# A recurrent-memory attention loop: the second softmax product split over two engines, a V copy moved ahead of a product, and one group of Q sums moved

## The chip, the cores and the metric

The kernel runs on one core of a Trainium2 chip. The metric is device time in microseconds (us) of one execution, compared as the median of several. Five engines matter: PE (TensorE, matmuls; its weight loads are shown as PEld), DVE (VectorE), ACT (ScalarE), POOL (GpSimd) and SP (SyncE, which issues the DMAs). Each runs its own instructions in order; they wait for each other by semaphores.

## The reference

The input of 2048 rows of 512 is normalised and cut into 64 segments of 32 rows. Each segment is attended to by 32 heads of 128 together with 8 memory rows, and the first 8 rows of the attention's output are the memory of the next segment, so the segments run one after the other. Behind it comes a gated MLP with a mixing over the 2048 rows.

```python
mem = mem0
for s in range(n_seg):
    h = concatenate([mem, xs], axis=1)
    q, k, v = h @ Wq, h @ Wk, h @ Wv            # 32 heads of 128
    p = softmax(where(mask, q @ k.T * scale, -1e9))
    o = (p @ v) @ Wo
    mem = o[:, :M, :]
    outs.append(o[:, M:, :])
# then: z = gelu(x @ w_in); g = w_sp @ layernorm(z2) + b_sp; out = (z1 * g) @ w_out
```

## The kernel before

**A list of operations.** Python code adds operations to an emitter, each with the tokens it reads and writes (`("E", b)` is the softmax numerator of head half `b`, `("V", b, h)` a half of that half's V). The emitter works out which semaphores an operation must wait for. An instruction carries one wait; each further wait is an instruction of its own on that engine. Each engine runs its operations in the order in which they were added. A POOL operation always waits for the POOL operation ahead of it.

**One segment.** The loop `for s in range(NSEG)` adds one segment at a time. The 32 heads are worked as two halves, `b` = 0 and 1, of 16. The large products on PE are split in fours: four matmuls, one in each column quarter of the array, for one 128-row chunk `dc` of the 512 input columns; a four of 512 columns costs PE one stream of 512 columns. When two fours that follow one another use the same chunk, the second keeps ("holds") the weights of the first (they show under line 501 instead of 500). In program order a segment is:

1. `QK` (through `tile_mm`, lines 500 and 501): fours for the Q and K sums. `QK(s, b, mi, dcs, first, last, held)` adds the fours of half `b`, `mi` 0 for Q and 1 for K, chunks `dcs`. Chunks 0 and 1 need the first half of the mem rows, chunks 2 and 3 the second.
2. In the middle of them `mem_out(s - 1, 1)` (line 702) transposes the second half of the last segment's mem rows with tiny matmuls; an ACT copy (line 707) puts them where the fours of chunks 2 and 3 read them.
3. `QK_evac`: ACT copies a finished PSUM bank to `Tst` (line 537), DVE transposes it into `QT` or `KT` (line 549). `mask_put` (DVE, line 561) writes the mask into the score bank. `K1` sums K of the second half in two 256-column parts, with `K1_copy` on ACT (line 527) and `K1_transpose` on DVE (line 534).
4. `S_half(s, b)` (lines 571 and 577): scores; `sm_exp` on ACT (line 585); `V_half` fours; `sm_sums` (lines 592, 501); `sm_ln` and `sm_rcp` on ACT (lines 603, 607) give the reciprocal `R`.
5. The softmax product `sm_norm` multiplies the first 160 columns of `E` by `R` (line 611), `sm_normx` the 64 columns of the ext part, which belong to the memory rows' neighbours of a whole row block (line 617, always DVE). `V_evac` copies V out of PSUM (DVE line 637, ACT line 635). An operation that reads a PSUM bank waits for another engine's read of that bank that was added before.
6. Filler work for PE (sums for later segments, lines 437, 418, 500 with `hTe`, or 797), then `PV_half(s, 0)` and `PV_half(s, 1)`: 16 small matmuls (line 645) and 4 for the ext part (line 651, which also read `Vx`, loaded by DMA a segment ahead), `cT_evac`, the output product `Wo`, `part_evac`, `mem_out(s, 0)`.

The order of step 5 is written out by hand: `sm_norm(0)` on POOL, then on DVE `sm_normx(0)`, `V_evac(1, (0,))`, `sm_norm(1)`, `sm_normx(1)`, with the other half of V's copy on ACT.

**The planner.** PE's instructions come in blocks of 256 (`FETCH`). `plan` looks four segments ahead, works out where in each segment a block ends, gives penalties to some places (`weight_of`), and chooses how many of a segment's fours reload weights instead of holding them, four more instructions each, to move the ends. `WAITS` and a term per segment count the separate wait instructions.

Of the kernel before, what the change touches and what calls it, by code (L numbers as in the profile page):

```python
# [10 lines left out]
ALU = mybir.AluOpType  # L11
# [158 lines left out]
def fast_path(nc, st, keep, A_x, A_mem0, A_Wq, A_Wk, A_Wv, A_Wo, A_seg_len, B_w_in, B_w_sp, B_b_sp, B_w_out, out):  # L170
# [9 lines left out]
    DC = D // 128  # L180
# [16 lines left out]
    def sb(name, shape, dt):  # L197
        return st.enter_context(nc.sbuf_tensor("f_" + name, shape, dt))
# [23 lines left out]
    NVX = 3  # L222
    Vx = sb("Vx", [128, NVX, 2, 128], BF)
    Vs = sb("Vs", [128, 2, 512], BF)
    E_sb = sb("E_sb", [128, 2, 224], BF)
    R_sb = sb("R_sb", [128, 2, 160], F32)
# [9 lines left out]
    ones = sb("ones", [128, 128], BF)  # L236
# [30 lines left out]
    def PB(b):  # L267
        return ("ps", b)
# [4 lines left out]
    pe_count = [0]  # L273
# [214 lines left out]
    PVB = (0, 1, 6, 7)  # L488
# [17 lines left out]
    def QK(s, b, mi, dcs, first, last, held=None):  # L506
        ws = (w_q, w_k)[mi]
        bank = QKB[(b, mi)]
        sl = slot(s)
        for dc in dcs:  # L510
            for c in range(4):
                rhs = ws[:, dc, :].rearrange("p (h c i) -> p c h i", c=4, i=32)[:, c, 16 * b:16 * b + 16, :]
                pe(lambda e, dc=dc, c=c, rhs=rhs: tile_mm(e, ps[32 * c:32 * c + 32, bank, :], hT[:, sl, dc, :], rhs,
                                                          dc == first, dc == last, c, dc == held), n=2 - (dc == held),
                   reads=[("hTx", (s // 4) % 3), ("hTm", s, dc // 2), ("W", mi, 2 * b), ("W", mi, 2 * b + 1)], writes=[PB(bank)])
# [67 lines left out]
    def sm_exp(b):  # L583
        bank = SBK[b]
        act(lambda e: e.activation(out=E_sb[:, b, :], in_=ps[:, bank, 0:224], func=ACT.Exp, scale=scale, bias=SHIFT),  # L585
            reads=[PB(bank)], writes=[("E", b), ("Ex", b)])

    def sm_sums(b):
        bank = SBK[b]
        for c in range(4):  # L590
            q = slice(32 * c, 32 * c + 32)
            pe(lambda e, q=q, c=c: e.matmul(ps[q, bank, 224:384], lhsT=ones[:, q], rhs=E_sb[:, b, 0:160], start=True, stop=False,  # L592
                                            skip_group_check=True, tile_position=(0, 32 * c)),
               reads=[("E", b), "ones"], writes=[PB(bank)])
        for c in range(4):
            q = slice(32 * c, 32 * c + 32)
            pe(lambda e, q=q, c=c: tile_mm(e, ps[q, bank, 224:384].rearrange("p (g q) -> p g q", q=40)[:, :, 0:16], ones[:, q],
                                           E_sb[:, b, 160:224].rearrange("p (g q) -> p g q", q=16), False, True, c, True), n=1,
               reads=[("Ex", b), "ones"], writes=[PB(bank)])
# [7 lines left out]
        act(lambda e: e.activation(out=R_sb[:, b, :], in_=R_sb[:, b, :], func=ACT.Exp, scale=-1.0, bias=RBIAS),  # L607
            reads=[("R", b)], writes=[("R", b)])

    def sm_norm(b, on):  # L610
        on(lambda e: e.tensor_tensor(out=E_sb[:, b, 0:160], in0=R_sb[:, b, :], in1=E_sb[:, b, 0:160], op=ALU.mult),
           reads=[("R", b), ("E", b)], writes=[("E", b)])

    def sm_normx(b):
        ev = E_sb[:, b, 160:224].rearrange("p (g q) -> p g q", q=16)
        rv = R_sb[:, b, :].rearrange("p (g q) -> p g q", q=40)[:, :, 0:16]
        dve(lambda e: e.tensor_tensor(out=ev, in0=rv, in1=ev, op=ALU.mult), reads=[("R", b), ("Ex", b)], writes=[("Ex", b)])

    def V_half(s, b, dcs=range(DC), held=None):
        bank = VB[b]  # L620
        sl = slot(s)
        last = 2 if b and s else DC - 1
        for dc in dcs:
            for c in range(4):
                c0 = (16 * b + 4 * c) * DH
                pe(lambda e, dc=dc, c=c, c0=c0: tile_mm(e, ps[32 * c:32 * c + 32, bank, :], hT[:, sl, dc, :], w_v[:, dc, c0:c0 + 512],
                                                        dc == 0, dc == last, c, dc == held), n=2 - (dc == held),
                   reads=[("hTx", (s // 4) % 3), ("hTm", s, dc // 2), ("W", 2, 2 * b), ("W", 2, 2 * b + 1)], writes=[PB(bank)])

    def V_evac(b, hs=(0, 1), eng="dve"):  # L630
        bank = VB[b]
        cs = slice(256 * hs[0], 256 * hs[-1] + 256)
        wr = [("V", b, h) for h in hs]
        if eng == "act":
            act(lambda e: e.activation(out=V_sb[:, b, cs], in_=ps[:, bank, cs], func=ACT.Copy), reads=[PB(bank)], writes=wr)
        else:
            dve(lambda e: e.tensor_copy(out=V_sb[:, b, cs], in_=ps[:, bank, cs]), reads=[PB(bank)], writes=wr)  # L637

    def PV_half(s, b):
        xb = s % NVX  # L640
        for g in range(4):
            for c in range(4):
                q = slice(32 * c, 32 * c + 32)
                c0 = 160 * b + 40 * g
                pe(lambda e, q=q, c=c, g=g, c0=c0: e.matmul(  # L645
                    ps[:, PVB[c], c0:c0 + 40], lhsT=V_sb[q, b, g * 128:(g + 1) * 128], rhs=E_sb[q, b, g * 40:(g + 1) * 40],
                    start=(g == 0), stop=False, skip_group_check=True, tile_position=(32 * c, 0)),
                    reads=[("V", b, g // 2), ("E", b)], writes=[PB(PVB[c])])
        for c in range(4):
            q = slice(32 * c, 32 * c + 32)  # L650
            pe(lambda e, q=q, c=c: e.matmul(  # L651
                ps[:, PVB[c], 160 * b:160 * b + 160].rearrange("p (g q) -> p g q", q=40)[:, :, 0:16], lhsT=Vx[q, xb, b, :],
                rhs=E_sb[q, b, 160:224].rearrange("p (g q) -> p g q", q=16),
                start=False, stop=True, skip_group_check=True, tile_position=(32 * c, 0)),
                reads=[("Vx", xb), ("Ex", b)], writes=[PB(PVB[c])])
# [41 lines left out]
    def mem_out(s, half):  # L697
        bank = GB[half]
        for dc in range(2 * half, 2 * half + 2):
            for c in range(4):  # L700
                c0 = dc * 128 + 32 * c
                pe(lambda e, dc=dc, c=c, c0=c0: e.matmul(ps[32 * c:32 * c + 32, bank, dc * M:(dc + 1) * M], lhsT=part[:, s % 8, c0:c0 + 32],  # L702
                                                         rhs=G_sb[:, :], start=True, stop=True, skip_group_check=True, tile_position=(0, 32 * c)),
                   reads=[("part", s % 8, half), "G"], writes=[PB(bank)])
        d2 = slice(2 * half, 2 * half + 2)
        src = ps[:, bank, 2 * half * M:(2 * half + 2) * M].rearrange("p (dc c) -> p dc c", c=M)
        act(lambda e: e.activation(out=hT[:, slot(s + 1), d2, 0:M], in_=src, func=ACT.Copy),  # L707
            reads=[PB(bank)], writes=[("hTm", s + 1, half)])
# [292 lines left out]
           reads=[("z2p", r, hf) for r in range(r0, r1) for hf in range(2)],  # L1001
           writes=[("z2", r, hf) for r in range(r0, r1) for hf in range(2)], after=[after])

    FETCH, FETCH0, WAITS = 256, 191, 15
    spare = [0]

    def weight_of(place):
# [6 lines left out]
    def plan(s, start, depth=4):  # L1014
        n = 588 + 24 * (s % 4 == 2) + 8 * (s >= 3 * CK)
        best = None
        for k in range(9):
            c = 10 * block_cost(start, 4 * k, n) + k
            if depth > 1:
                c += plan(s + 1, start + n + 4 * k + 2, depth - 1)[0]  # L1020
            if best is None or c < best[0]:
                best = (c, k)
        return best

    def hold(x):
        if spare[0] > 0:
            spare[0] -= 1
            return None
        return x
# [5 lines left out]
    for s in range(NSEG):  # L1035
# [12 lines left out]
        if s == 4:  # L1048
            load_xe(3, 1)

        spare[0] = plan(s, pe_count[0] + WAITS + 2 * s)[1] if s else 0
        QK(s, 0, 0, (0,), 0, 3)
        QK(s, 0, 1, (0,), 0, 2, hold(0))
        if s > 0:
            mem_out(s - 1, 1)
        QK(s, 0, 1, (1,), 0, 2)
        QK(s, 0, 0, (1, 2, 3), 0, 3, hold(1))
        QK_evac(s, 0, 0)
# [1 line left out]
        QK(s, 0, 1, (3, 2), 0, 2, hold(3))  # L1060
        QK_evac(s, 0, 1)
        mask_put(1)
        QK(s, 1, 0, (2, 0, 1, 3), 2, 3, hold(2))
        lastop["q"] = em.by_eng["pe"][-1]
        QK_evac(s, 1, 0)
        K1(s, 0, 3, True, False, bool(hold(True)))
# [35 lines left out]
        if s == 0:  # L1102
            for n in range(2, 4):
                start_v(n)
            V_half(s, 1)
            sm_sums(1)
        else:
            V_half(s, 1, (3, 1), 3)
            sm_sums(1)
            V_half(s, 1, (2,))  # L1110
        lastop["v"] = em.by_eng["pe"][-1]
        sm_ln(1)
        sm_rcp(1)
# [8 lines left out]
        if s + 1 < NSEG:  # L1122
            qx_copy(s + 1)
            lastop["x"] = xops[s + 1] = em.by_eng["pool"][-1]
        sm_norm(0, pool)
        sm_normx(0)
        V_evac(1, (0,))
        V_evac(1, (1,), "act")
        sm_norm(1, dve)
        sm_normx(1)  # L1130
        if s == 0:
            for n in range(4, 8):
# [90 lines left out]
        if c2 + 8 <= s < c3:  # L1223
            k, m = (s - c2 - 8) // 2, s % 2
# [6 lines left out]
        if s in (c3 + 5, c3 + 7, c3 + 11, c3 + 13):  # L1231
            dc = (c3 + 5, c3 + 7, c3 + 11, c3 + 13).index(s)
# [203 lines left out]
    for tb in range(NTB):  # L1436
        for fb in range(len(ACC) if tb == 0 else 0, FB):
            if tb == 0:
                bank = 5 + fb % 3
            else:  # L1440
                bank = gcnt % 2
# [786 lines left out]
```

## Time and profile before

| | us |
|---|---|
| median of 3 runs (lowest, highest) | 845.12 (843.77, 845.2) |
| the profiled execution | 842.99 |
| its span, first to last instruction | 841.3 |
| PE busy in the span | 827.7 (98%) |
| DVE busy | 524.0 (62%) |
| ACT busy | 469.1 (56%) |
| POOL busy | 127.4 (15%) |

Timeline rows read: start in us, length in us, engine, line, operation, output and inputs, how many instructions were merged, and in brackets how long the engine idled before and what ended that. Where several instructions are merged, the length is from the first's start to the last's end. Rows of groups by line read: line, engine, operation, names, shape, count, then busy time in us, mean of one in ns and idle time before them. The ends of matmuls are modelled, and matmuls overlap, so their spacing is read from start to start. The granted TensorE clock is 1.000 throughout.

### The profile page before, as it was taken

The numbers are of one execution on the slowest core, as the hardware profiler recorded it, in microseconds if no ns is written. First come the engines' busy times: TensorE is split into PE (matmuls) and PEld (weight loads), VectorE is DVE, ScalarE is ACT, GpSimd is POOL, SyncE is SP. The second block draws the span as 40 slices with busy tenths as digits, with TensorE's granted clock in tenths as the row PEclk, the third lists the DMA queues.
The fourth block names the chain that finished last, engine by engine and source line by source line (L and its number), as shares of the span: only waits on it lengthen the run. The fifth ranks groups of instructions, "written<-read, shape, count | busy, mean of one in ns | idle before, by whom it ended". The sixth has DMA issues, their size and how long they took to land.

```text
span 841.3 us, 44814 instructions
## 1 busy us (share of the span) xinstructions
PE 827.7 (98%) x21935; PEld 427.5 (51%) x18845; DVE 524.0 (62%) x1320; ACT 469.1 (56%) x1251; POOL 127.4 (15%) x340
## 2 busy tenths in 40 slices
PE   6999999999999999999999999999999999999998
PEld 6754445555555554555555545455555544444443
DVE  3555667666666666676766676666666666554443
ACT  3456566766666666666666666666666676500000
POOL 5111111111111111111211111111111123200000
PEclk9999999999999999999999999999999999999999
DMA  9962222222222232121323232333323298033001
GB/s 319 379 220 55 78 61 64 71 58 68 56 54 49 59 48 66 38 68 48 82 42 88 54 71 54 84 77 87 85 69 81 74 276 286 1 113 109 30 14 40
DMA packets 111252, 77.29 MB, mean 92 GB/s; under 512 B 64840, under 2 KB 100688, under 8 KB 111056
## 3 DMA queue, kind: packets, MB, share of 16 engines
q1 hardware_dynamic: 111056, 74.36, 31.1%
q8 instruction: 162, 2.65, 1.3%
q14 instruction: 34, 0.28, 0.1%
HBM read 42.38 MB, written 21.59 MB: 76 GB/s over the span
## 4 chain that ended last, share of the span: by engine, by line
PE 97%; DMA 1%; SPq 1%; issue 0%; DVE 0%; ACT 0%
PE f_ps L500 45%; PE f_ps L501 13%; PE f_ps L1303 12%; PE f_ps L729 4%; PE f_ps L1296 3%; PE f_ps L1420 3%; PE f_ps L645 3%; PE f_ps L437 2%; PE f_ps L797 2%; PE f_ps L418 2%; PE f_ps L571 1%; DMA f_arena<-in_A_Wk_dram 1%; PE f_ps L592 1%; PE f_ps L443 1%; PE f_ps L702 1%; PE f_ps L651 1%
## 5 line engine op out<-in xcount | busy, mean ns | idle before, releaser
L500 PE MATMUL f_ps<-f_arena,f_hT 128*32 128x512 bf16 (+1 forms) x4832 | 356.2, 356 | 0.3
L500 PEld LDWEIGHTS f_ps<-f_arena,f_hT 128*32 128x32 bf16 x4832 | 119.8, 96 | 155.6 <-issue 63.5
L501 PE MATMUL f_ps<-f_arena,f_hT 128*32 128x512 bf16 (+1 forms) x2336 | 186.7, 334 | 0.0
L537 ACT ACTIVATE f_Tst<-f_ps 128x512 bf16<-128x512 f32 x228 | 129.4, 597 | 60.3 <-PE f_ps L500 60.3
L500 PE MATMUL f_ps<-f_arena,f_cT 128*32 128x256 bf16 x3844 | 129.1, 272 | 0.9 <-ACT f_cT L664 0.5
L500 PEld LDWEIGHTS f_ps<-f_arena,f_cT 128*32 128x32 bf16 x3844 | 94.4, 96 | 29.0 <-ACT f_cT L664 19.1
L1303 PE MATMUL f_ps<-f_arena 128*128 128x512 bf16 x448 | 100.9, 379 | 0.0
L549 DVE STREAM_TRANSPOSE f_QT<-f_Tst 128x256 uint32<-128x256 uint32 x128 | 57.1, 446 | 67.5 <-ACT f_Tst L537 67.5
L637 DVE CAST f_V_sb<-f_ps 128x512 bf16<-128x512 f32 (+1 forms) x128 | 71.0, 555 | 41.9 <-PE f_ps L500 41.9
L666 DVE TENSOR_SCALAR f_cT<-f_ps 128x320 bf16<-128x320 f32 x128 | 56.9, 486 | 27.8 <-PE f_ps L651 27.8
L1303 PEld LDWEIGHTS f_ps<-f_arena 128*128 128x128 bf16 x448 | 43.7, 98 | 52.6
L585 ACT ACTIVATE f_E_sb<-f_ps 128x224 bf16<-128x224 f32 x128 | 46.2, 361 | 36.4 <-PE f_ps L577 36.4
L695 DVE CAST f_part<-f_ps 128x256 bf16<-128x256 f32 x64 | 27.2, 425 | 61.9 <-PE f_ps L500 61.9
L556 POOL COPY f_QT<-f_arena 128x128 uint32<-128x128 uint32 x64 | 18.7, 292 | 298.4 <-PE f_ps L577 298.3
L664 ACT ACTIVATE f_cT<-f_ps 128x320 bf16<-128x320 f32 x128 | 49.0, 435 | 22.6 <-PE f_ps L651 22.6
L707 ACT ACTIVATE f_hT<-f_ps 128x16 bf16<-128x16 f32 x126 | 23.2, 184 | 53.6 <-PE f_ps L702 53.2
L1309 DVE TENSOR_TENSOR f_arena<-f_ps,f_arena 128x512 f32<-128x512 f32 x28 | 19.3, 690 | 52.9 <-PE f_ps L1303 52.9
L561 DVE CAST f_ps<-f_mask 128x224 f32<-128x224 bf16 x128 | 47.0, 367 | 0.0
L607 ACT ACTIVATE f_R_sb<-f_R_sb 128x160 f32<-128x160 f32 x128 | 43.1, 337 | 4.0
L527 ACT ACTIVATE f_Tst<-f_ps 128x256 bf16<-128x256 f32 x128 | 42.1, 381 | 3.7
L686 POOL COPY f_cTx<-f_cT 128x256 bf16<-128x256 bf16 x64 | 25.4, 396 | 121.0 <-DVE f_cT L666 121.0
L693 ACT ACTIVATE f_part<-f_ps 128x256 bf16<-128x256 f32 x64 | 24.6, 384 | 31.4 <-PE f_ps L500 31.4
(123 smaller groups left out, 1202.1 us busy)
## 6 DMA issues: line engine op xcount, KB each, us to landing
wT_d<-f_wst SPq DMA_DIRECT2D x64, 128.0 KB, 2.3
f_arena<-wT_d SPq DMA_DIRECT2D x32, 256.0 KB, 4.9
f_arena<-in_A_Wq_dram SPq DMA_DIRECT2D x4, 1024.0 KB, 8.7
f_arena<-in_A_Wk_dram SPq DMA_DIRECT2D x4, 1024.0 KB, 14.0
f_arena<-in_A_Wv_dram SPq DMA_DIRECT2D x4, 1024.0 KB, 14.6
f_arena<-in_A_Wo_dram SPq DMA_DIRECT2D x8, 512.0 KB, 9.6
f_Vx<-vext_d SPq DMA_DIRECT2D x63, 64.0 KB, 2.7
vext_d<-f_Vs SPq DMA_DIRECT2D x24, 128.0 KB, 2.0
```

The costliest lines, as they stand in the source:

```text
L500: return e.matmul(out, lhsT=lhsT, rhs=rhs, start=start, stop=stop, skip_group_check=True, tile_position=(0, 32 * c))
L501: return e.add_instruction(mybir.InstMatmult(name=nc.get_next_instruction_name(), ins=[e.lower_ap(rhs), e.lower_ap(lhsT)], outs=[e.lower_a ...
L527: act(lambda e: e.activation(out=Tst[:, 1, 256 * k:256 * k + 256].rearrange("p (gi r) -> p gi r", r=2), in_=ps[:, bank, 0:256].rearrange(" ...
L537: act(lambda e: e.activation(out=Tst[:, tb, :].rearrange("p (C gi r) -> p C gi r", C=2, r=2), in_=ps[:, bank, :].rearrange("p (C r gi) -> ...
L549: dve(lambda e: e.transpose(out=dst, in_=Tst[:, mi, :].bitcast(U32)), reads=[("T", mi, 0), ("T", mi, 1)], writes=wr)
L561: dve(lambda e: e.tensor_copy(out=ps[:, bank, 0:224], in_=mask[:, :]), reads=["mask"], writes=[PB(bank)])
L585: act(lambda e: e.activation(out=E_sb[:, b, :], in_=ps[:, bank, 0:224], func=ACT.Exp, scale=scale, bias=SHIFT), reads=[PB(bank)], writes=[ ...
L607: act(lambda e: e.activation(out=R_sb[:, b, :], in_=R_sb[:, b, :], func=ACT.Exp, scale=-1.0, bias=RBIAS), reads=[("R", b)], writes=[("R", b)])
L637: dve(lambda e: e.tensor_copy(out=V_sb[:, b, cs], in_=ps[:, bank, cs]), reads=[PB(bank)], writes=wr)
L664: act(lambda e: e.activation(out=dst, in_=src, func=ACT.Copy, scale=UNSC), reads=[PB(PVB[c])], writes=[("cT", c)])
L666: dve(lambda e: e.tensor_scalar(out=dst, in0=src, scalar1=UNSC, scalar2=None, op0=ALU.mult), reads=[PB(PVB[c])], writes=[("cT", c)])
L1303: pe(lambda e: e.matmul(ps[:, bank, 0:TB], lhsT=z2[:, sc, fb * 128:(fb + 1) * 128], rhs=wTb[tb % 2][:, :, sc, :], start=(n == 0), stop=(n ...
```

## The change

The token `("E", b)` is cut in two, columns 0 to 119 and 120 to 159. The product of the second half is made by DVE for the first part and by POOL for the second. DVE's copy of the first half of V of `b` = 1 is added ahead of the ext product of `b` = 0. `QK(s, 1, 0, ...)`, the Q sums of the second half, begins with its chunk 0 right behind `mem_out(s - 1, 1)` instead of in the middle of its own group. PE's wait for the `Vx` load moves from the ext matmul of `PV_half` to the last V four, and its wait for the second part of V by one matmul. The planner counts one separate wait a segment instead of two, and one more at the start.

```diff
-            reads=[PB(bank)], writes=[("E", b), ("Ex", b)])
+            reads=[PB(bank)], writes=[("E", b, 0), ("E", b, 1), ("Ex", b)])
...
-    def sm_norm(b, on):
-        on(lambda e: e.tensor_tensor(out=E_sb[:, b, 0:160], in0=R_sb[:, b, :], in1=E_sb[:, b, 0:160], op=ALU.mult),
-           reads=[("R", b), ("E", b)], writes=[("E", b)])
+    def sm_norm(b, on, hs=(0, 1)):
+        q = slice((0, 120)[hs[0]], (120, 160)[hs[-1]])
+        tok = [("E", b, h) for h in hs]
+        on(lambda e: e.tensor_tensor(out=E_sb[:, b, q], in0=R_sb[:, b, q], in1=E_sb[:, b, q], op=ALU.mult),
+           reads=[("R", b), *tok], writes=tok)
...
-    def V_half(s, b, dcs=range(DC), held=None):
+    def V_half(s, b, dcs=range(DC), held=None, also=()):
...
-                   reads=[("hTx", (s // 4) % 3), ("hTm", s, dc // 2), ("W", 2, 2 * b), ("W", 2, 2 * b + 1)], writes=[PB(bank)])
+                   reads=[("hTx", (s // 4) % 3), ("hTm", s, dc // 2), ("W", 2, 2 * b), ("W", 2, 2 * b + 1), *(also if c == 3 else ())], writes=[PB(bank)])
...
-                    reads=[("V", b, g // 2), ("E", b)], writes=[PB(PVB[c])])
+                    reads=[("V", b, g // 2), ("E", b, g // 3), *([("V", b, 1)] if (g, c) == (1, 3) else [])], writes=[PB(PVB[c])])
...
-    FETCH, FETCH0, WAITS = 256, 191, 15
+    FETCH, FETCH0, WAITS, STEP = 256, 191, 16, 1
...
-                c += plan(s + 1, start + n + 4 * k + 2, depth - 1)[0]
+                c += plan(s + 1, start + n + 4 * k + STEP, depth - 1)[0]
...
-        spare[0] = plan(s, pe_count[0] + WAITS + 2 * s)[1] if s else 0
+        spare[0] = plan(s, pe_count[0] + WAITS + STEP * s)[1] if s else 0
         QK(s, 0, 0, (0,), 0, 3)
         QK(s, 0, 1, (0,), 0, 2, hold(0))
         if s > 0:
             mem_out(s - 1, 1)
+        QK(s, 1, 0, (0,), 0, 3)
         QK(s, 0, 1, (1,), 0, 2)
         QK(s, 0, 0, (1, 2, 3), 0, 3, hold(1))
         QK_evac(s, 0, 0)
...
         QK_evac(s, 0, 1)
         mask_put(1)
-        QK(s, 1, 0, (2, 0, 1, 3), 2, 3, hold(2))
+        QK(s, 1, 0, (2, 1, 3), 0, 3, hold(2))
...
-            V_half(s, 1, (2,))
+            V_half(s, 1, (2,), also=[("Vx", s % NVX)])
...
         sm_norm(0, pool)
+        V_evac(1, (0,))
         sm_normx(0)
-        V_evac(1, (0,))
         V_evac(1, (1,), "act")
-        sm_norm(1, dve)
+        sm_norm(1, dve, (0,))
+        sm_norm(1, pool, (1,))
         sm_normx(1)
```

More of the change, by code (lines that the diff above doesn't have):

```diff
@@ L593, in sm_sums @@
                                             skip_group_check=True, tile_position=(0, 32 * c)),
-               reads=[("E", b), "ones"], writes=[PB(bank)])
+               reads=[("E", b, 0), ("E", b, 1), "ones"], writes=[PB(bank)])
         for c in range(4):
```

## The prediction, made before the change was run

> **What bounds the kernel now.** I read the page first, for its span and its chain of waits, then the groups of instructions by line on PE, and then the timeline of single segments, because what the change moves is far smaller than any group of the page.
>
> ```profile
> span 841.3 us, 44814 instructions
> ...
> PE 97%; DMA 1%; SPq 1%; issue 0%; DVE 0%; ACT 0%
> ...
> f_Vx<-vext_d SPq DMA_DIRECT2D x63, 64.0 KB, 2.7
> ```
>
> PE makes up 97% of the chain that ends last, so only two things count: PE's own work, which the change does not touch, and the short waits between PE's instructions, repeated in the 63 segments that have a predecessor (one Vx load each). The first is the Q and K stage, here in the segment that begins at 314.58.
>
> ```profile
> 314.58 0.22 PE L702 MATMUL f_ps<-f_G_sb,f_part 128*32 128x8 bf16 x8
> ...
> 314.86 0.39 PE L501 MATMUL f_ps<-f_arena,f_hT 128*32 128x512 bf16 x4
> ...
> 315.09 0.12 PEld L500 LDWEIGHTS f_ps<-f_arena,f_hT 128*32 128x32 bf16 x8 [0.36 <-ACT f_hT L707]
> 315.09 0.61 PE L500 MATMUL f_ps<-f_arena,f_hT 128*32 128x512 bf16 x8
> ...
> 315.76 1.09 ACT L537 ACTIVATE f_Tst<-f_ps 128x512 bf16<-128x512 f32 x2 [0.72 <-PE f_ps L500]
> ...
> 316.39 0.45 DVE L549 STREAM_TRANSPOSE f_QT<-f_Tst 128x256 uint32<-128x256 uint32 x1 [1.86 <-ACT f_Tst L537]
> 316.76 0.37 DVE L561 CAST f_ps<-f_mask 128x224 f32<-128x224 bf16 x1
> ...
> 317.03 0.42 DVE L549 STREAM_TRANSPOSE f_KT<-f_Tst 128x256 uint32<-128x256 uint32 x1
> ...
> 317.06 0.60 ACT L537 ACTIVATE f_Tst<-f_ps 128x512 bf16<-128x512 f32 x1 [0.21 <-PE f_ps L500]
> ...
> 317.38 0.37 DVE L561 CAST f_ps<-f_mask 128x224 f32<-128x224 bf16 x1
> ...
> 317.69 0.45 DVE L549 STREAM_TRANSPOSE f_QT<-f_Tst 128x256 uint32<-128x256 uint32 x1
> 317.70 0.27 PE L571 MATMUL f_ps<-f_QT,f_KT 128*32 128x40 bf16 x16
> ...
> 318.13 0.59 DVE L534 STREAM_TRANSPOSE f_KT<-f_Tst 128x128 uint32<-128x128 uint32 x2
> ...
> 318.80 0.27 PE L571 MATMUL f_ps<-f_QT,f_KT 128*32 128x40 bf16 x16
> ```
>
> The mem rows' transposition (L702) ends in an ACT copy, and the first four that reads these rows, at 315.09, has waited for it. DVE then runs back to back from the first transpose at 316.39, each operation beginning about 0.08 before the one ahead ends (316.39+0.45 against 316.76). The two score products (L571) need its results: that at 317.70 the transpose that ends at 317.45, that at 318.80 the pair that ends at 318.72.
>
> The second stage is the product with V, in the same segment.
>
> ```profile
> 319.69 0.39 PE L500 MATMUL f_ps<-f_arena,f_hT 128*32 128x512 bf16 x4
> ...
> 319.91 1.04 PE L500 MATMUL f_ps<-f_arena,f_hTe 128*32 128x512 bf16 x16
> ...
> 320.13 0.23 DVE L617 TENSOR_TENSOR f_E_sb<-f_R_sb,f_E_sb 128x64 bf16<-128x64 f32 x1
> 320.24 0.49 POOL L611 TENSOR_TENSOR f_E_sb<-f_R_sb,f_E_sb 128x160 bf16<-128x160 f32 x1 [0.74 <-ACT f_R_sb L607]
> 320.27 0.42 DVE L637 CAST f_V_sb<-f_ps 128x256 bf16<-128x256 f32 x1
> 320.32 0.34 ACT L607 ACTIVATE f_R_sb<-f_R_sb 128x160 f32<-128x160 f32 x1
> 320.69 0.33 DVE L611 TENSOR_TENSOR f_E_sb<-f_R_sb,f_E_sb 128x160 bf16<-128x160 f32 x1
> 320.72 0.38 ACT L635 ACTIVATE f_V_sb<-f_ps 128x256 bf16<-128x256 f32 x1
> ...
> 320.88 0.27 PE L645 MATMUL f_ps<-f_E_sb,f_V_sb 32*128 32x40 bf16 x16
> 320.93 0.22 DVE L617 TENSOR_TENSOR f_E_sb<-f_R_sb,f_E_sb 128x64 bf16<-128x64 f32 x1
> ...
> 321.07 0.31 PE L645 MATMUL f_ps<-f_E_sb,f_V_sb 32*128 32x40 bf16 x16
> ...
> 321.23 0.20 PE L651 MATMUL f_ps<-f_E_sb,f_Vx 32*128 32x64 bf16 x4
> 321.35 0.62 PE L729 MATMUL f_ps<-f_arena,f_cTx 128*32 128x512 bf16 x8
> ```
>
> ```profile
> 549.99 1.12 PE L797 MATMUL f_ps<-f_arena 128*32 128x448 bf16 x20
> ...
> 551.04 0.27 PE L645 MATMUL f_ps<-f_E_sb,f_V_sb 32*128 32x40 bf16 x16
> ...
> 551.45 0.61 PE L729 MATMUL f_ps<-f_arena,f_cTx 128*32 128x512 bf16 x8
> ```
>
> From the first V product to L729 PE takes 0.47 here and 0.41 in the later segment, whose longer filler work (five fours, not four) lets the products be ready. So 0.06 is all that this stage can give. The segments with a filler of four 512-column fours are 36:
>
> ```profile
> L500 PE MATMUL f_ps<-f_arena,f_hTe 128*32 128x512 bf16 x576 | 37.3, 379 | 0.0
> ```
>
> (576 matmuls, 16 in each.) The wait ahead of the first V product goes down to POOL's product in the profile. But in both segments it starts about 0.11 after the filler's last four has streamed (319.91 and four times 0.22 is 320.78; 549.99 and five times 0.19 is 550.93), whatever POOL does, so I do not count on it. The Trainium skill, "TensorEngine Tiling (Array Packing)", Key Properties, says that a change of tiling mode drains TensorE; the forms 128\*32 and 32\*128 on either side agree, and by it these 0.11 stay.
>
> **One four moved behind the mem rows' transposition.** The four's work is unchanged: same four loads and four matmuls, same weights, and its PSUM bank is free. It puts 0.22 between L702 and the four at 315.09. That four now comes 0.23 after the one at 314.86, not 0.217 ((1.04 less 0.39) by 3), and its weights could not be loaded ahead, which I put at 0.01: gain 0.03, in 63 segments 1.9 us.
>
> The price is that the first half's Q sums end 0.19 later (0.22 less 0.03), and ACT's copy at 315.76 and all of DVE's chain start from them. With the spacings of the rows: transpose 316.58, mask 316.95 (0.37), K transpose 317.22 (0.27) to 317.64, mask 317.57 (0.35), second transpose 317.84 (0.27: it no longer waits for ACT's copy, which ends at 317.66), the last pair 318.21 (0.37). The pair took 0.59 while it also waited for ACT, and two of them 0.08 overlapped take 0.54, so it ends between 318.75 and 318.80; I take 318.77. From DVE's end to PE's start goes 0.05 (320.69+0.33 to 321.07). The first score product can then start at 317.69 where PE comes at 317.67, 0.03 early: **the gain is spent there.** The second can start at 318.82 against 318.80 now, with 0.01 for weights not loaded ahead: 0.03 late. Behind it PE's sums, ACT's exponent and everything after wait, so nothing absorbs it: 63 by 0.03 is **+1.9 us**. Bounds: −1.9 (DVE keeps up) and +3.8 (pair at 318.80, 0.06).
>
> **V copy ahead of the ext product.** The copy waits for the four at 319.69, which ends at 320.08; it can start at 320.13, not 320.27, and end at 320.55. ACT's copy of the other V half, which followed DVE's at 320.72, can start when ACT is done at 320.66. But the ext product, until now started at 320.13 ahead of POOL's, would start at 320.47 in the middle of POOL's, which reads SBUF from 320.24 to 320.73. What that does, one odd segment shows, where POOL ran late:
>
> ```profile
> 540.51 0.49 POOL L611 TENSOR_TENSOR f_E_sb<-f_R_sb,f_E_sb 128x160 bf16<-128x160 f32 x1 [1.03 <-ACT f_R_sb L603]
> 540.67 0.51 DVE L611 TENSOR_TENSOR f_E_sb<-f_R_sb,f_E_sb 128x160 bf16<-128x160 f32 x1
> ```
>
> DVE's product took 0.51 instead of 0.33 and ended 0.18 after POOL's. The ext product is 0.11 shorter (0.22 against 0.33), so it ends some 0.08 after POOL's, at 320.81. Its own reader, the ext matmul of the first half, comes at about 321.00 and is not late; the next on DVE is.
>
> **Second product shared.** DVE's 120 columns cost 0.28 (0.33 less 40 columns at 0.11/96) and start 0.08 before the ext product ends: 320.73 to 321.01, against 321.02 now. So the V product at 321.07 gains 0.01 at most, not 0.06. POOL's 40 columns start 0.08 after its first product, as in this pair:
>
> ```profile
> 255.61 0.22 POOL L367 TENSOR_SCALAR f_rs<-f_mv 128x1 f32<-128x1 f32 x1 [2.51 <-DVE f_mv L366]
> 255.91 0.57 POOL L369 TENSOR_TENSOR f_rs<-f_rs,f_mhalf 128x1 f32<-128x1 f32 x1
> ```
>
> at 320.81, and last between 0.12 (a quarter of 0.49) and 0.29 (0.22 for one column and 40/160 of the rest); the row at 0.22 speaks for 0.29. With DVE reading until 320.93 they end between 320.93 and 321.22, at PE 0.05 later; the last sixteenth of the V product that needs them comes at 321.15. DVE's last ext product starts at 320.93, may wait for POOL's 40 columns, and ends between 321.15 and 321.30: 321.20 to 321.35 on PE, 321.23 now. I take **0** for both edits, with −0.06 and +0.12 as bounds: −2.2 to +4.3 in the 36 segments.
>
> **The rest.** The wait for the Vx load moves forward to the V four at 319.69; the load lands in 2.7 us and was issued a segment before, so it costs nothing (the whole 2.7 if it were issued in its own segment). One PE wait instruction a segment goes, and the planner's constants follow it; where instruction blocks end moves. A stall of that kind is
>
> ```profile
> 383.68 0.11 PEld L500 LDWEIGHTS f_ps<-f_arena,f_cT 128*32 128x32 bf16 x5 [0.32 <-issue]
> ```
>
> Three more or fewer of them are 1.0 us; I take 0.
>
> **Sum.** +1.9 on the profiled execution's 842.99 (span 841.3) is 844.9. The median of the runs shown stands 2.1 above that execution, so 845.1 becomes **847.0**.
>
> **Rivals.** (a) *It works as drawn.* DVE keeps up at the score products and the ext product is not held: −1.9 and −2.2, 841.0; only the four's gain gives 843.2, only the V stage's, with the chain late, 844.8. For it: 0.06 is really lost at 321.07. Against it: DVE's back-to-back rows and the row at 540.67. (b) *Slower: the port is held for the whole instruction.* POOL's 40 columns then start at 321.01, end at 321.30 and reach PE at 321.35, not 321.15, and the last ext product comes after them: 0.20 in 36 segments, about 0.08 in the other 27, where the longer filler brings PE 0.08 (five times 0.19 less four times 0.22) or more later, 9.4 in all; with the chain's 1.9, 856. It decides if the two engines' second products meet. If POOL took its turn first the price is the same (DVE's product would end at 321.23). Against it: at 320.13 and 320.24 the two spans overlap and POOL still takes 0.49. The Trainium skill, "SBUF — State Buffer", Who interferes with whom, states this rule: a DVE instruction with two SBUF inputs and a GpSimd one that reads SBUF exclude each other, the first to issue for its whole duration. The row at 540.67 agrees with the exclusion, the overlap at 320.24 not with the whole duration. (c) *The edits do not show* (POOL and DVE end within the same few hundredths, block ends decide): 845.1, give or take 1.
>
> **Numbers.** Likeliest 0.45, (a) 0.29, (b) 0.14, (c) 0.12. A difference under 0.2%, 1.7 us, cannot be told from none: 843.4 to 846.8. The likeliest, by its bounds 845.5 to 849, gives 0.16 same and 0.29 slower; (a) 0.23 faster and 0.06 same; (b) slower; (c) 0.04, 0.05, 0.03. Together 0.27, 0.27, 0.46. The range 842.0 to 852.0 leaves out (a) with both gains and most of (b).
>
> **What would show it.** In the changed timeline: no wait for ACT at the third four after L702; DVE's last K transposes ending 0.04 or more later after L702 than now, and the second score product waiting for DVE; the ext product stretched to 0.3 or more beside POOL's; the second V product no earlier. Wrong if the ext product keeps 0.23, if segments are shorter than 9.94, or if PE waits for POOL in the second V product.

## The result, and the profile after

The changed kernel takes 847.51 us (median of 11 runs, 847.07 to 848.72) where the kernel before, on the same chip, takes 845.12: the ratio is 1.0034, 95% interval 1.0026 to 1.0041. It is slower by about 2.4 us by the medians, 2.9 by the ratio, and the interval lies wholly above 1. The profiled execution of after took 847.51, with a span of 845.7; that of before took 842.99, with 841.3. The lines of the code below the softmax have moved by two: 611, 617, 637, 645, 651, 702, 707 and 729 of before are 613, 619, 639, 647, 653, 704, 709 and 731 now.

From the page of after, its first line and the shares of the chain that ended last:

```profile
span 845.7 us, 44920 instructions
...
PE 95%; DMA 2%; SPq 1%; ACT 1%; issue 0%; POOL 0%; DVE 0%
```

PE is the chain still, so the loss has to be in short waits again. The timeline of after, Q and K stage, in the segment that begins at 316.71. The segment of the prediction begins at 314.58, so 2.13 is to be taken off to lay the rows on those of before:

```profile
316.71 0.21 PE L704 MATMUL f_ps<-f_G_sb,f_part 128*32 128x8 bf16 x8
...
316.77 0.60 PE L500 MATMUL f_ps<-f_arena,f_hT 128*32 128x512 bf16 x8
316.99 0.18 ACT L709 ACTIVATE f_hT<-f_ps 128x16 bf16<-128x16 f32 x1
317.20 0.39 PE L501 MATMUL f_ps<-f_arena,f_hT 128*32 128x512 bf16 x4
...
317.42 0.60 PE L500 MATMUL f_ps<-f_arena,f_hT 128*32 128x512 bf16 x8
...
318.70 0.45 DVE L549 STREAM_TRANSPOSE f_QT<-f_Tst 128x256 uint32<-128x256 uint32 x1 [2.05 <-ACT f_Tst L537]
...
319.07 0.37 DVE L561 CAST f_ps<-f_mask 128x224 f32<-128x224 bf16 x1
...
319.35 0.42 DVE L549 STREAM_TRANSPOSE f_KT<-f_Tst 128x256 uint32<-128x256 uint32 x1
...
319.82 0.17 PEld L571 LDWEIGHTS f_ps<-f_QT,f_KT 128*32 128x32 bf16 x16
319.83 0.28 PE L571 MATMUL f_ps<-f_QT,f_KT 128*32 128x40 bf16 x16
...
319.96 0.43 DVE L549 STREAM_TRANSPOSE f_QT<-f_Tst 128x256 uint32<-128x256 uint32 x1
...
320.31 0.56 DVE L534 STREAM_TRANSPOSE f_KT<-f_Tst 128x128 uint32<-128x128 uint32 x2
...
320.92 0.17 PEld L571 LDWEIGHTS f_ps<-f_QT,f_KT 128*32 128x32 bf16 x16
320.93 0.27 PE L571 MATMUL f_ps<-f_QT,f_KT 128*32 128x40 bf16 x16
```

The first four that reads the mem rows, the third behind the transposition in before, is now the fourth behind L704 and starts 0.22 after the one ahead (317.20 and 317.42): the wait for ACT's copy is gone. DVE's first transpose comes 0.18 later than before (1.99 after the segment's start, was 1.81), and the rest of its chain runs without a gap. The pair of last transposes ends at 320.87, 4.16 after the start, where it was 4.14. The second score product starts 4.22 after the start, as before. What PE saved in front, it now waits for at the first score product, whose weights load 0.01 ahead of it (319.82 and 319.83). Before, they had loaded 0.10 ahead; these two rows of the timeline of before belong to the score products at 317.70 and 318.80:

```profile
317.60 0.27 PEld L571 LDWEIGHTS f_ps<-f_QT,f_KT 128*32 128x32 bf16 x16
...
318.77 0.19 PEld L571 LDWEIGHTS f_ps<-f_QT,f_KT 128*32 128x32 bf16 x16
```

The second score product had waited for DVE before, too: its weights loaded 0.05 after the transposes' end, and 0.03 ahead of it.

The timeline of after, product with V, same segment:

```profile
322.05 1.04 PE L500 MATMUL f_ps<-f_arena,f_hTe 128*32 128x512 bf16 x16
...
322.38 0.88 POOL L613 TENSOR_TENSOR f_E_sb<-f_R_sb,f_E_sb 128x160 bf16<-128x160 f32 x2 [0.74 <-ACT f_R_sb L607]
...
322.61 0.33 DVE L619 TENSOR_TENSOR f_E_sb<-f_R_sb,f_E_sb 128x64 bf16<-128x64 f32 x1
...
322.73 0.38 ACT L637 ACTIVATE f_V_sb<-f_ps 128x256 bf16<-128x256 f32 x1
...
322.87 0.27 DVE L613 TENSOR_TENSOR f_E_sb<-f_R_sb,f_E_sb 128x120 bf16<-128x120 f32 x1
...
323.02 0.27 PE L647 MATMUL f_ps<-f_E_sb,f_V_sb 32*128 32x40 bf16 x16
323.06 0.28 DVE L619 TENSOR_TENSOR f_E_sb<-f_R_sb,f_E_sb 128x64 bf16<-128x64 f32 x1
...
323.20 0.32 PE L647 MATMUL f_ps<-f_E_sb,f_V_sb 32*128 32x40 bf16 x16
...
323.40 0.21 PE L653 MATMUL f_ps<-f_E_sb,f_Vx 32*128 32x64 bf16 x4
...
323.54 0.62 PE L731 MATMUL f_ps<-f_arena,f_cTx 128*32 128x512 bf16 x8
```

POOL's row holds both of its products: 160 columns and 40, done at 323.26. DVE's first ext product lies beside the first of them and its last ext product beside the second; the first takes 0.33 and the last 0.28, where both took 0.22 to 0.23. The last one ends at 323.34, and the ext matmul that reads it starts at 323.40, 6.69 after the segment's start, where it was 6.65 (321.23 less 314.58). From the first V product to L731 PE takes 0.52, was 0.47. ACT's copy of V's second part ends at 323.11, 6.40 after the segment's start, where it was 6.52 (320.72 and 0.38, less 314.58).

Single matmuls, which these rows merge, show two more waits inside the second V product (medians of the 36 segments, from the segment's start). In before PE stands there until V's second part is copied: ACT's copy ends at 6.526 and the ninth of the 16 matmuls starts at 6.581. In after this copy comes early enough, but PE now stands there for POOL's 40 columns: they end at 6.548, and the thirteenth matmul starts at 6.605 where the ninth had started at 6.551. This wait costs nothing further, since the ext matmul behind it waits longer, for DVE's last ext product.

That these rows are typical, the groups by line and form show (count, then busy us and mean ns of one), of before:

```profile
L617 DVE TENSOR_TENSOR f_E_sb<-f_R_sb,f_E_sb 128x64 bf16<-128x64 f32 x128 | 28.4, 222 | 4.3
...
L571 PEld LDWEIGHTS f_ps<-f_QT,f_KT 128*32 128x32 bf16 x2048 | 28.9, 96 | 0.9 <-issue 0.6
```

and of after:

```profile
L619 DVE TENSOR_TENSOR f_E_sb<-f_R_sb,f_E_sb 128x64 bf16<-128x64 f32 x128 | 38.6, 302 | 0.0
...
L613 POOL TENSOR_TENSOR f_E_sb<-f_R_sb,f_E_sb 128x160 bf16<-128x160 f32 x64 | 31.3, 490 | 54.3 <-ACT f_R_sb L607 53.3 <-ACT f_R_sb L603 1.0
...
L571 PEld LDWEIGHTS f_ps<-f_QT,f_KT 128*32 128x32 bf16 x2048 | 22.2, 95 | 8.7 <-issue 0.6
L613 POOL TENSOR_TENSOR f_E_sb<-f_R_sb,f_E_sb 128x40 bf16<-128x40 f32 x64 | 20.1, 313 | 7.4 <-ACT f_R_sb L607 2.1 <-ACT f_V_sb L637 0.4
L613 DVE TENSOR_TENSOR f_E_sb<-f_R_sb,f_E_sb 128x120 bf16<-128x120 f32 x64 | 17.6, 274 | 0.2 <-ACT f_R_sb L607 0.2
```

The ext products grew from 222 to 302 ns in the mean of all 128. POOL's 160 columns did not grow (489 before). The score products' weight loads idle 8.7 us instead of 0.9.

**Where the time went.** Each segment's timeline gives four places: the second half's mem-row transposition (the start), the second score product S1, the second ext matmul X1, and the output product L729 behind it (L731 in after). These are medians, in us, for the segments with a filler of four 512-column fours (29 of the 36, those with neighbours of their kind) and, behind a slash, for the 14 with five 448-column fours. "e1" to "e9" are the experiments below.

| kernel | start to S1 | S1 to X1 | X1 to L729 | segment |
|---|---|---|---|---|
| before | 4.214 | 2.431 / 2.430 | 0.125 / 0.138 | 9.947 / 9.934 |
| after | 4.221 | 2.466 / 2.466 | 0.138 / 0.138 | 10.003 / 9.976 |
| e1, four alone | 4.222 | 2.429 / 2.429 | 0.125 / 0.138 | 9.952 / 9.939 |
| e2, after without the four | 4.213 | 2.468 / 2.467 | 0.138 / 0.138 | 9.996 / 9.976 |
| e3, e2, whole product on DVE | 4.213 | 2.442 / 2.445 | 0.138 / 0.138 | 9.972 / 9.949 |
| e4, e2, ext product first | 4.213 | 2.436 / 2.435 | 0.138 / 0.138 | 9.963 / 9.937 |
| e5, both moved waits alone | 4.214 | 2.434 / 2.434 | 0.136 / 0.137 | 9.962 / 9.948 |
| e6, a smaller four | 4.184 | 2.429 / 2.430 | 0.124 / 0.139 | 9.915 / 9.932 |
| e7, e2, share of 80 columns | 4.213 | 2.501 / 2.502 | 0.138 / 0.138 | 10.031 / 10.004 |
| e8, Vx wait alone | 4.214 | 2.429 / 2.429 | 0.125 / 0.141 | 9.949 / 9.954 |
| e9, V wait alone | 4.214 | 2.433 / 2.433 | 0.137 / 0.137 | 9.960 / 9.935 |

Eleven other segments grew by about 0.006 (nine of them, medians: 10.061 to 10.067), and one, with four 448-column fours, from 9.892 to 9.943; the last segment has none behind it to end its length. So the segments of after cost 36 times 0.056, 14 times 0.042, 11 times 0.006 and once 0.05: 2.7 us, against 2.4 by the medians and 2.9 by the ratio. In the last column behind the slash a median is drawn up in e5, e6 and e8, where about half of the 14 segments hold a stall, which I put down to the ends of instruction blocks; their undisturbed segments are 9.933 to 9.937, 9.900 to 9.907 and 9.933 to 9.935.

### The profile page after: what moved, and what is told of

The parts are those of the page before. It is cut to its first block, busy times and chain, and to the rows that moved or that the text cites. A ratio compares the mean times of both kernels' runs of the same rounds, so it can differ in the third digit from the quotient of the medians.

```text
span 845.7 us, 44920 instructions
## 1 busy us (share of the span) xinstructions
PE 830.3 (98%) x21945; PEld 425.1 (50%) x18877; DVE 516.4 (61%) x1320; ACT 465.1 (55%) x1251; POOL 147.5 (17%) x404
## 4 chain that ended last, share of the span: by engine, by line
PE 95%; DMA 2%; SPq 1%; ACT 1%; issue 0%; POOL 0%; DVE 0%
PE f_ps L500 44%; PE f_ps L501 13%; PE f_ps L1307 11%; PE f_ps L731 4%; PE f_ps L1424 3%; PE f_ps L1300 3%; PE f_ps L647 3%; PE f_ps L437 2%; PE f_ps L799 2%; DMA f_arena<-in_A_Wk_dram 2%; PE f_ps L571 2%; PE f_ps L418 1%; PE f_ps L592 1%; PE f_ps L443 1%; PE f_ps L704 1%; PE f_ps L653 1%
## 5 line engine op out<-in xcount | busy, mean ns | idle before, releaser
L500 PEld LDWEIGHTS f_ps<-f_arena,f_hT 128*32 128x32 bf16 x4864 | 122.2, 95 | 151.3 <-issue 63.2
L613 POOL TENSOR_TENSOR f_E_sb<-f_R_sb,f_E_sb 128x160 bf16<-128x160 f32 (+1 forms) x128 | 51.4, 401 | 61.7 <-ACT f_R_sb L607 55.4
```

Source lines behind the costliest of these rows:

```text
L500: return e.matmul(out, lhsT=lhsT, rhs=rhs, start=start, stop=stop, skip_group_check=True, tile_position=(0, 32 * c))
L613: on(lambda e: e.tensor_tensor(out=E_sb[:, b, q], in0=R_sb[:, b, q], in1=E_sb[:, b, q], op=ALU.mult), reads=[("R", b), *tok], writes=tok)
```

## The experiments

All ratios are against runs of the kernel before on the same chip.

**e1: the moved four alone.** The kernel before with this part only:

```diff
             mem_out(s - 1, 1)
+        QK(s, 1, 0, (0,), 0, 3)
         QK(s, 0, 1, (1,), 0, 2)
...
-        QK(s, 1, 0, (2, 0, 1, 3), 2, 3, hold(2))
+        QK(s, 1, 0, (2, 1, 3), 0, 3, hold(2))
```

> The kernel before with only the four of Q sums moved behind the mem rows' transposition; waits, planner and V stage as before. If the loss lies in the V stage (POOL and DVE shutting each other out), this kernel keeps the 0.01 a segment that the changed trace shows at the score products: 845.6, ratio about 1.0006. If the loss is DVE's late transposes, as the prediction's sum had it (0.03 a segment): 847.0, 1.0022. If both are wrong and the four is a gain: 843.2, 0.998.

Measured: 845.39 against 844.29, ratio 1.0014 (1.0004 to 1.0024). S1 is 0.008 later than before and the segment 0.005 longer. The timeline shows the place of the wait that is gone, and that of the one that took its place:

```profile
315.79 0.22 PE L702 MATMUL f_ps<-f_G_sb,f_part 128*32 128x8 bf16 x8
...
316.51 0.60 PE L500 MATMUL f_ps<-f_arena,f_hT 128*32 128x512 bf16 x8
...
318.92 0.17 PEld L571 LDWEIGHTS f_ps<-f_QT,f_KT 128*32 128x32 bf16 x16
318.92 0.28 PE L571 MATMUL f_ps<-f_QT,f_KT 128*32 128x40 bf16 x16
```

What follows: the four brings nothing and costs little, 36 times 0.005, 14 times 0.005 and 11 times 0.002, 0.3 us. The rest of its 1.1 us lies in no segment's median and is not explained.

**e2: the whole change without the four.** The diff of e1 taken back from the changed kernel.

> The changed kernel with the four of Q sums back in its old place; all else as changed. If the V stage makes the loss: segments 0.045 longer than before where the filler has four fours, 0.035 where it has five of 448, in all 2 us: 847.2, ratio 1.0024. If the four made it: 845.1, 1.000.

Measured: 848.15 against 844.29, ratio 1.0038 (1.0023 to 1.0053). S1 to X1 stays at 2.468 and X1 to L729 at 0.138. So the loss lies in the V stage's edits and the moved waits.

**e3: e2 with the second product whole on DVE.**

```diff
-        sm_norm(1, dve, (0,))
-        sm_norm(1, pool, (1,))
+        sm_norm(1, dve)
```

> As the changed kernel without the four's move, and with the second softmax product whole on DVE again; the V copy stays ahead of the ext product. If POOL's first product shuts out the ext product (first exclusion), DVE's product starts 0.05 late and the last ext product too, but no second exclusion follows: the V stage's last ext matmul 0.03 late instead of 0.045, about 1 us in all, 846.2, ratio 1.0012, and the first ext product still takes 0.33. If only POOL's 40 columns cost: 845.1, 1.000.

Measured: 845.25 against 844.29, ratio 1.0018 (1.0006 to 1.003). What is left of the V stage's edits is the V copy ahead of the ext product, with the moved waits. Its timeline (segment from 315.29):

```profile
320.94 0.49 POOL L613 TENSOR_TENSOR f_E_sb<-f_R_sb,f_E_sb 128x160 bf16<-128x160 f32 x1 [0.74 <-ACT f_R_sb L607]
...
321.18 0.33 DVE L619 TENSOR_TENSOR f_E_sb<-f_R_sb,f_E_sb 128x64 bf16<-128x64 f32 x1
...
321.44 0.31 DVE L613 TENSOR_TENSOR f_E_sb<-f_R_sb,f_E_sb 128x160 bf16<-128x160 f32 x1
...
321.67 0.21 DVE L619 TENSOR_TENSOR f_E_sb<-f_R_sb,f_E_sb 128x64 bf16<-128x64 f32 x1
```

The first ext product is held as in after (0.33, ending 0.08 after POOL's 321.43); the last one, with no POOL product beside it, is back at 0.21. S1 to X1 is 2.442, so 0.026 of the 0.037 that e2 lost there (2.468 against 2.431) come with POOL's 40 columns.

**e4: e2 with the ext product ahead of the V copy again.**

```diff
-        V_evac(1, (0,))
         sm_normx(0)
+        V_evac(1, (0,))
```

> As the changed kernel without the four's move, and with the ext product ahead of the V copy again; the second product stays shared. If the exclusion is the cause, the first ext product is back at 0.23, DVE's 120 columns start at the old time, so the second V product starts 0.04 earlier, but the last ext product still waits for POOL's 40 columns: V stage between 0.01 shorter and 0.03 longer than before, 844.8 to 846.2. If the order of V copy and ext product is without effect: as the changed kernel without the four, 847.2.

Measured: 846.46 against 844.29, ratio 1.0023 (1.0012 to 1.0035). Its timeline (segment from 315.36):

```profile
320.91 0.23 DVE L619 TENSOR_TENSOR f_E_sb<-f_R_sb,f_E_sb 128x64 bf16<-128x64 f32 x1
321.02 0.85 POOL L613 TENSOR_TENSOR f_E_sb<-f_R_sb,f_E_sb 128x160 bf16<-128x160 f32 x2 [0.74 <-ACT f_R_sb L607]
...
321.47 0.28 DVE L613 TENSOR_TENSOR f_E_sb<-f_R_sb,f_E_sb 128x120 bf16<-128x120 f32 x1
...
321.50 0.38 ACT L637 ACTIVATE f_V_sb<-f_ps 128x256 bf16<-128x256 f32 x1
...
321.67 0.28 DVE L619 TENSOR_TENSOR f_E_sb<-f_R_sb,f_E_sb 128x64 bf16<-128x64 f32 x1
```

The first ext product is free (0.23) and the second V product starts 0.04 earlier than in before (6.45 after the start, was 6.49, medians): here the share does what it is drawn for. But X1 is at 2.436 all the same, for two waits take the gain back and end together. The last ext product is held by POOL's 40 columns (0.28, ending at 321.95, 0.08 after POOL), and X1 starts 0.058 after it. And inside the second V product PE still waits for V's second part, whose copy on ACT ends at 321.88, 6.52 after the start as in before: the matmul behind that wait starts at 6.580 in e4 and in e5. The segments are those of e5, which has neither edit: the share is worth nothing alone, too, and by these rows would gain nothing even without the hold, for in e5, where nothing holds the ext product, X1 is at 2.434. A kernel with ACT's copy early and the ext products not held was not run.

**e7: e2 with the share at 80 columns each.**

```diff
-        q = slice((0, 120)[hs[0]], (120, 160)[hs[-1]])
+        q = slice((0, 80)[hs[0]], (80, 160)[hs[-1]])
...
-                    reads=[("V", b, g // 2), ("E", b, g // 3), *([("V", b, 1)] if (g, c) == (1, 3) else [])], writes=[PB(PVB[c])])
+                    reads=[("V", b, g // 2), ("E", b, g // 2), *([("V", b, 1)] if (g, c) == (1, 3) else [])], writes=[PB(PVB[c])])
```

> As the changed kernel without the four's move, with POOL's part of the second product doubled, 80 of 160 columns. If DVE's last ext product waits for POOL's part, it ends a further 0.09 later (40 columns at 0.0022), and the V stage with it: segments 0.08 to 0.13 longer than before, 5 us in all, ratio 1.006. If POOL's part were hidden and the V copy's place alone cost: as without the four, 1.0025 to 1.004.

Measured: 848.52 against 844.52, ratio 1.0043 (1.0028 to 1.0058). From its groups by form:

```profile
L619 DVE TENSOR_TENSOR f_E_sb<-f_R_sb,f_E_sb 128x64 bf16<-128x64 f32 x128 | 43.3, 338 | 0.0
...
L613 POOL TENSOR_TENSOR f_E_sb<-f_R_sb,f_E_sb 128x80 bf16<-128x80 f32 x64 | 22.3, 348 | 7.4 <-ACT f_R_sb L607 2.1 <-ACT f_V_sb L637 0.4
L613 DVE TENSOR_TENSOR f_E_sb<-f_R_sb,f_E_sb 128x80 bf16<-128x80 f32 x64 | 14.9, 232 | 0.2 <-ACT f_R_sb L607 0.2
```

POOL's second product grew by 35 ns (313 to 348), X1 came 33 ns later (2.468 to 2.501) and the segments grew by 28 to 35. DVE's own product is 42 ns shorter (274 to 232) and that helps nothing. So X1 hangs on the end of POOL's second product, through the ext product that ends 0.08 behind it. Twice the columns cost POOL only a ninth more, and that ninth is the whole of the further loss; the doubled share had been expected to cost more than that.

**e5, e8, e9: the moved waits.** e5 is the kernel before with both of PE's moved waits and the planner's constants, e8 with the `Vx` wait and the constants, e9 with the V wait alone:

```diff
-                    reads=[("V", b, g // 2), ("E", b)], writes=[PB(PVB[c])])
+                    reads=[("V", b, g // 2), ("E", b), *([("V", b, 1)] if (g, c) == (1, 3) else [])], writes=[PB(PVB[c])])
```

> Of the change only the moved Vx and V waits and the planner's constants; both softmax products, the V copy and the four as before. If only the exclusion costs: segments 9.95 and 9.93 as before, ratio 1.000. If where instruction blocks end costs, as the fourth experiment suggests (its segments are only 0.6 us longer in all, its time 1.9): up to 1.3 us more than before, ratio 1.0015, all of it in single odd segments.

> The kernel before with only PE's wait for the Vx load moved from the ext product of the first half to the last V four, and the planner's constants that go with it. The run with both moved waits and nothing else was longer by 0.015 in the 36 segments with a four-four filler, 0.011 to 0.013 of it between the second ext product and the output product behind it, and by 0.0010 as a ratio. Theory A (the wait ahead of a matmul inside the second V product costs it): this kernel keeps the segments of before, 9.947 median, and the gap of 0.125 from the second ext product to the output product; 845, within 0.5 of before. Theory B (the Vx wait, or the block ends that follow its count, costs it): the segments are 9.962 and the gap 0.136; some 0.5 to 0.8 slower than before.

> The kernel before with only PE's wait for the second part of V taken one matmul earlier, the last of the second sixteenth's group instead of the first of the third's; the planner is untouched. Theory A (this wait's place costs it): segments of 9.962 in the 36 with a four-four filler, the second ext product to the output product 0.136 instead of 0.125, 0.5 to 0.8 slower than before. Theory B (the Vx wait costs it): as before, 9.947 and 0.125, within 0.5 of before.

Measured: e5 845.49 against 844.52, ratio 1.0010 (1.0002 to 1.0019); e8 845.74 against 844.61, 1.0015 (1.0005 to 1.0025); e9 844.79 against 844.61, 1.0005 (0.9995 to 1.0016). Of the two theories on record for e8 and e9 each is right in part, at different places. In these kernels the 0.012 between X1 and L729 are the V wait's: e9 has them and e8 has not; 36 times 0.013 is 0.5 us, within e9's interval. The single matmuls show how. The wait ends when it did in before (the matmul behind it starts at 6.58 in both), but it stands one matmul earlier, so nine instead of eight of the 16 are left behind it. The last of the four ext matmuls starts at 6.668 instead of 6.655, and L729 follows it by 0.114 in both, within 0.001.

In after this is not what happens. V's second part is there at 6.40, before PE asks for it. Yet X1 to L729 takes 0.138 there, too, and in e2, e3 and e7, where ACT's copy is as early: in all four X1 waits for the held ext product, and the output product follows the last ext matmul by 0.128 where in before it is 0.114. What lengthens that step stays open.

And e8 is slower by about 1.1 us although its undisturbed segments are those of before. In its profiled execution the excess over the medians, summed over the segments of the table and the nine, is 3.5 us, in before's 1.9: with one wait instruction a segment fewer, the blocks end elsewhere. That is one execution of each, so this size is a reading, and the cause is argued and not shown.

**e6: a smaller four behind the mem rows' transposition.** The kernel before with chunk 0 of `K1`'s second part, a four of 256 columns, in that place:

```diff
             mem_out(s - 1, 1)
+        if s > 0:
+            K1(s, 1, 0, True, False, False)
         QK(s, 0, 1, (1,), 0, 2)
...
-        K1(s, 1, 3, True, False, bool(hold(True)))
+        K1(s, 1, 3, s == 0, False, bool(hold(True)))
...
-        K1(s, 1, 0, False, False, bool(hold(True)))
+        if s == 0:
+            K1(s, 1, 0, False, False, bool(hold(True)))
...
-        n = 588 + 24 * (s % 4 == 2) + 8 * (s >= 3 * CK)
+        n = 592 + 24 * (s % 4 == 2) + 8 * (s >= 3 * CK)
...
-        for k in range(9):
+        for k in range(8):
```

> The kernel before, with another four moved behind the mem rows' transposition: a 256-column four of K1 (part 1, chunk 0), half as long, so that the first half's Q sums and DVE's chain come 0.08 late instead of 0.19. If the four's gain was spent at the first score product because DVE's chain is 0.16 short of slack, here it stays: segments 0.025 shorter, 1.6 us in all, 843.5, ratio 0.998. If a four behind the transposition gains nothing in itself: 1.000 or above.

Measured: 843.09 against 844.52, ratio 0.9978 (0.9969 to 0.9988): faster than both kernels. Its timeline:

```profile
315.11 0.22 PE L702 MATMUL f_ps<-f_G_sb,f_part 128*32 128x8 bf16 x8
...
318.12 0.25 PEld L571 LDWEIGHTS f_ps<-f_QT,f_KT 128*32 128x32 bf16 x16
318.21 0.27 PE L571 MATMUL f_ps<-f_QT,f_KT 128*32 128x40 bf16 x16
...
318.67 0.55 DVE L534 STREAM_TRANSPOSE f_KT<-f_Tst 128x128 uint32<-128x128 uint32 x2
...
319.27 0.19 PEld L571 LDWEIGHTS f_ps<-f_QT,f_KT 128*32 128x32 bf16 x16
319.30 0.27 PE L571 MATMUL f_ps<-f_QT,f_KT 128*32 128x40 bf16 x16
```

The weights of the first score product load 0.09 ahead of it again, and the pair of transposes ends 4.11 after the start (4.14 in before): DVE is not late. S1 comes 0.030 sooner and the segment is 0.032 shorter (9.947 to 9.915). The wait at the mem rows needed a cover of some hundredths, and this one pushes DVE's first transpose back by 0.08 where the whole four does by 0.19 (medians). The predicted gain of 0.03 at the mem-row wait was right; it is kept where DVE's chain is not made late.

## Why the prediction was right, and where it was not

The forecast of 847.0 came out within 0.5 us, slower, as said. Part of that is luck: three of its terms were wrong in size and made up for each other.

- **The moved four, +0.03 a segment, +1.9 us: mis-sized.** The mechanism was as told: the gain at the mem-row wait is spent at the first score product, and the second waits for DVE. But the lateness there was +0.008, and the four alone costs 0.3 us by its segments. The last pair of transposes was put at 0.37 behind the transpose ahead of it, since a transpose took 0.45; that transpose took 0.43 here and the pair began 0.35 behind it (319.96 and 320.31). The pair ends 0.02 later in the segment than before, not 0.05, and the score product follows its weights by 0.01 (320.92 and 320.93) where before it was 0.03, so nothing was lost there either. Lateness that is the difference of two sums of six spacings cannot be had to 0.03 from rows rounded to 0.01.
- **V copy ahead and second product shared, 0: mis-sized, and the largest miss.** Each step but one was right: taken from the segment's start the first ext product was put to end at 6.23, and ended at 6.23; DVE's 120 columns were put from 6.15 to 6.43, and ran from 6.16 to 6.43; the last ext product was put to start at 6.35, and did. The second V product came no earlier, as said (6.49 in both, medians). Then "may wait for POOL's 40 columns" gave an end between 6.57 and 6.72, and 0 was taken for the product on PE although the middle of that is 0.04 later than before. The miss has two sources. POOL's 40 columns take 0.31, above the upper bound of 0.29, and the last ext product ends 0.08 after them, as the prediction itself had worked out for the first one from the odd row at 540.67. Measured: S1 to X1 +0.035. The bounds of −0.06 to +0.12 held it.
- **Only 36 segments: wrong.** The same 0.036 was lost in the 14 segments with five 448-column fours, since what decides there in after is not when PE comes to the first V product but when the last ext product ends. X1 starts 0.058 behind that end where it waits for it (after, e2, e3, e4, e7) and 0.075 behind it in before, in both kinds of segment: 0.02 was to spare. In after the product ends 0.06 later in the segment. Together 50 times 0.036 is 1.8 us.
- **What the V stage can give, 0.06: read incompletely.** The difference between 0.47 and 0.41 was put down to the softmax products alone. PE also waits for ACT's copy of V's second part inside the second V product, and e4 beside e5 shows that a second V product 0.04 earlier gains nothing while that copy stays where it is.
- **The rest, 0 with 1.0 either way: nearly.** The `Vx` wait costs nothing where it stands. The V wait, which was given no cost of its own, costs 0.013 in 36 segments where it is moved alone (e9). After has the same 0.013 between X1 and the output product, 0.5 us, behind the held ext product; the prediction has no term for it. The excess of after's segments over their medians is some 0.7 us above that of before, by one execution each (2.6 and 1.9).

The rivals: (a) fell with e2 and e3, as the ext product is held. (b) wanted POOL's 40 columns to start only when DVE's product ends, at 323.14; they are done at 323.26 with 0.31 of length, so they started near 322.95, beside it. (c) fell: the segments are longer, in all kinds. Of the four signs named for the changed timeline, three came; of the transposes' the second score product does wait for DVE, but they end 0.02 later and not 0.04 or more. One of the three signs of being wrong came, too: PE waits for POOL's 40 columns in the second V product, by 0.02 to 0.03 (0.054 from the ninth matmul to the thirteenth, against 0.025 in e3). That wait is covered by the longer one for the ext product.

## What to carry to other kernels

A product moved from one engine to another is worth what its last reader gains, and not what the shorter product gains: look for what stands behind it on the same engine and reads beside the new neighbour, and for the other operand of the reader, which may come no earlier. A wait is filled with the smallest piece of work that covers it; a piece twice as long makes the chain behind it late and gives the gain back. A difference of a few hundredths in a chain of short operations should be carried as a range around its middle, and a "may wait" for another engine counted at its likely length, not at nothing.

## What the runs showed of the hardware

**DVE and POOL beside each other.** A DVE product of two SBUF inputs that starts while a POOL product runs does not end before it: in after, in e4 and in e7 the ext product ends 0.08 behind POOL's end (medians), whether it is stretched to 0.28 or to 0.33 (in e7 338 ns in the mean of all), while POOL's 160 columns keep 0.49. When DVE starts first, neither of the first products grows: in e4 0.23 from 320.91, with POOL's from 321.02 and 0.49 long. The second products of both engines overlap by more than 0.15; whether they grow by it no run shows, as none has POOL's short product with DVE idle. The Trainium skill, "SBUF — State Buffer", Who interferes with whom, has the two engines exclude each other on the ports that they share; the held ext products agree, and the overlaps where DVE is first show no whole-duration hold of POOL, as far as POOL's rough spans can tell.

**POOL's short products cost more than their share of columns.** 160 columns take 490 ns, 80 take 348 (e7) and 40 take 313 (283 in e4). So 80 columns fewer save 142 ns, and 40 fewer than that only 35. All the short ones ran beside a DVE product, so how much of the 313 is fixed and how much is waiting is not settled. Handing 40 columns over took 41 ns off DVE (328 in before to 287 in e4; 315 in e3 to 274 in after) and put 313 on POOL.
